# Fourier mixing and a tanh-shrink dense layer on one core: weight conversion in finer steps, with clamp and sums on other engines

## The chip, the cores and the metric

The kernel runs on one core of a Trainium2 chip. A core has five engines that work through their own instruction queues in order and meet only at semaphores: TensorE (PE, matrix products; its weight loads are PEld), VectorE (DVE), ScalarE (ACT), GpSimd (POOL) and SyncE (SP), which here only issues DMA transfers. ScalarE and GpSimd issue DMAs too. The metric is the device time of one execution in microseconds, the median of several runs; lower is better.

## The reference

The input `x` holds 8 batches of 3008 tokens with 256 channels. Every batch is filtered along the sequence in the frequency domain, and the result goes through two dense layers with h - tanh(h) between them:

```python
def _attn_ref(x, filt_r, filt_i):
    X = np.fft.rfft(x, axis=1)
    F = (filt_r + 1j * filt_i)[None, :, :]
    return np.fft.irfft(X * F, n=x.shape[1], axis=1).astype(np.float32)

def _moe_ref(x, w_in, w_out):          # x (24064, 256), w_in (256, 2048), w_out (2048, 256)
    h = x @ w_in
    g = h - np.tanh(h)
    return (g @ w_out).astype(np.float32)
```

The two weight matrices arrive as 64-bit floats, and the kernel reads them as pairs of 32-bit words: each weight's sign, exponent and mantissa are taken apart with integer operations and put together again as a 32-bit float.

## The kernel before

**Fourier part.** The transform of 3008 = 64 x 47 points is done in matrix products. For one batch, `first` (twelve steps, product `pf`, L255) reads x and writes `ct1` to memory; `middle` (seven groups `g` of rows) loads `a2` from `ct1` and a part of the filter (`ft`, from `filt_d`), multiplies (`pa`, L287), applies the filter on VectorE (L292 to L312), multiplies back (`pe`, L322) and writes `ct2`; `last` loads `e2` from `ct2` and makes the tokens of one group (`pu`, L419; `ut`, and the sums `tu` by `combine`). A batch has six groups of tokens.

**Dense part.** A round `U` is one quarter of the hidden channels for one group of tokens; four rounds make a group, 192 rounds make the kernel. Both layers use a scheme of seven products for a 2 x 2 block product: `wu` (first layer) and `wd` (second layer) hold seven blocks, four of which are sums of others, formed by `sums`; the token side is formed by `combine` (four subtractions). In the body for `U`, `up(U)` multiplies by `wu` into the banks x, y and z and gathers `h` with VectorE (L476, L493, L501, L509) and with copies on ScalarE (`s1`, `u2`, `u3`, L459); `shrink(U-1)` works through ScalarE (turn, bend, square: L524, L527, L530) and VectorE (L534), and ends with `combine` on GpSimd, which makes `t`; `down(U-2)` multiplies by `wd` (L578).

**What sets the order.** The order on every engine is the order in which Python emits the instructions. The steps are generators: at fixed places of `up`, `d`, `e`, `s` and `t` advance the other work by one step. `t(k)` for k = 0 to 4 issues stores, takes one step of the Fourier work of later batches if its place in the plan has come (`pos = 20 * c + 5 * u + k`; `planned` spreads the steps of `first` and `middle` over positions: `first(1)` from 6 to 20, `first(2)` from 20 to 34 and `middle(1)` from LEAD = 34 to LAG = 104), advances `late` by two steps, and `copies` (transfers that GpSimd issues to build `filt_d`) by one. `pf`, `pa`, `pe` and `pu` take turns in two banks, t and y; y is also the bank of the second product of `up`, read by L476.

**Weights.** A job is 128 x 512 weights, a quarter is two jobs and then `sums`. `converted` loads the raw words, takes mantissa (`it`), exponent (`pt`) and sign (`st`) on VectorE (L145, L146, L148), makes a float of the mantissa and shifts the exponent's bias on ScalarE (L157, L158), then on VectorE adds the low word (L160), clamps the exponent at 255 (L162), joins it with the sign (L164) and multiplies into the two or three destinations (L171). It yields four times. Three quarters (six jobs) are converted in the prologue by `convert`: four jobs before the loop over the groups of batch 0, two behind it. The other five quarters are converted by `weights_slow` in the first rounds, one job after the other. `sums` stands on GpSimd (L201 to L204), and so does `combine` for every group but the first.

**Buffers.** In the rounds a job's tiles borrow those of the Fourier work (`tiles1`: raw from `ft`, `it` from `xy`, `pt` from `nn`, `st` from `e1`, `ft` from `a2`); two raw loads are begun ahead. In the prologue the stores of `ct2` for batch 0 go through `e1` with two buffers.

Of the kernel before, what the change touches and what calls it, by code (L numbers as in the profile page):

```python
# [27 lines left out]
NX = NH // XH  # L28
# [62 lines left out]
def kernel(  # L91
# [26 lines left out]
    mats = cst.tile([KM, 6 * KM + 8 * KL], F32, name="mats_sb")  # L118
    exp_b = cst.tile([128, 1], F32, name="exp_b")
    groups = [(b, c) for b in range(BATCH) for c in range(NC)]  # L120
    count = cst.tile([1, 1], I32, name="count")
# [11 lines left out]

    def converted(tiles, src, dsts, queue, alone=False):
# [13 lines left out]
        V.tensor_scalar(out=st, in0=hi, scalar1=-2 ** 31, scalar2=None, op0=ALU.bitwise_and)  # L148
        yield

        if alone:
            V.tensor_scalar(out=ft, in0=it, scalar1=2.0 ** -20, scalar2=1.0,
                            op0=ALU.mult, op1=ALU.add)
            V.tensor_scalar(out=pt, in0=pt, scalar1=-896.0, scalar2=0.0,
                            op0=ALU.add, op1=ALU.max)
        else:
            ACT.activation(ft, it, AF.Identity, bias=1.0, scale=2.0 ** -20)  # L157
            ACT.activation(pt, pt, AF.Relu, bias=exp_b)  # L158
        yield
        V.scalar_tensor_tensor(out=ft, in0=lo, scalar=2.0 ** -52, in1=ft,  # L160
                               op0=ALU.mult, op1=ALU.add)
        V.tensor_scalar_min(pt, pt, 255.0)  # L162
        yield
        V.scalar_tensor_tensor(out=pt, in0=pt, scalar=23, in1=st,  # L164
                               op0=ALU.logical_shift_left, op1=ALU.bitwise_or)
        pt = pt.bitcast(F32)
        for cols, dst, sign in dsts:
            f, p = ft[:, cols], pt[:, cols]
            if len(dst.shape) == 3:
                f, p = (v.rearrange("p (h n) -> p h n", h=dst.shape[1]) for v in (f, p))  # L170
            V.scalar_tensor_tensor(out=dst, in0=f, scalar=sign, in1=p, op0=ALU.mult, op1=ALU.mult)  # L171
        yield
# [33 lines left out]
    def begun(tiles, job, alone=False, queue=nc.sync):  # L206
        j = converted(tiles, *job, queue, alone)
        next(j)
        return j

    def weights_slow(tiles, quarters):

        jobs = parts_of(quarters)
        began = [begun(tiles, job) for job in jobs[:2]]
        yield
        for k in range(len(jobs)):
            for _ in began[k]:
                yield
            if k + 2 < len(jobs):
                began.append(begun(tiles, jobs[k + 2]))  # L220
            if k % 2:
                sums(quarters[k // 2])
                yield

# [185 lines left out]
    def last(i, z):  # L410
# [101 lines left out]
    def shrink(U):  # L512
# [20 lines left out]
        def times(k):  # L533
# [216 lines left out]
    with tc.tile_pool(name="tr", bufs=2) as tr, tc.manual_schedule():  # L750

        def tiles1(k, dtype, n):

            tag, bufs = {"raw": ("ft", 2), "it": ("xy", 2), "pt": ("nn", 1), "st": ("e1", 2),
                         "ft": ("a2", 2)}[k]
            return tr.tile([128, n], dtype, tag=tag, bufs=bufs, name=k)

        with tc.tile_pool(name="pro", bufs=1) as pro, \
# [62 lines left out]
            f0 = pro.tile([128, NH, 128], F32, name="f0")  # L821
            V.memset(exp_b, 0.0)
            for t in filt:
                G.memset(t[0:SG, 2:4], 0.0)
# [16 lines left out]

            def convert(k):

                for _ in range(1 if k + 1 < len(jobs) else 0):
                    next(began[k + 1])
                for _ in began[k]:
                    pass
                if k % 2:
                    sums(k // 2)
                if k + 4 < len(jobs):  # L850
                    began.append(begun(tiles0, jobs[k + 4], queue=G))

# [17 lines left out]
            for g in range(last_g + 1):  # L870
# [30 lines left out]
        with tc.tile_pool(name="dn", bufs=2) as dn, \  # L901
# [49 lines left out]
            for U in range(total + 2):  # L951
# [24 lines left out]
                def e():  # L976

                    next(dw, None)

                def s():  # L980
# [3 lines left out]
                def t(k):  # L984
# [76 lines left out]
```

## Time and profile before

| | us |
|---|---|
| median of three runs (2797.88 to 2799.99) | 2798.9 |
| the profiled execution | 2804.2 |
| its span, first to last instruction | 2802.3 |

The busy time of the engines in stretches of the span (us), with the mean granted clock of TensorE and the share of time that the 16 DMA engines were busy:

| stretch | length | PE | DVE | ACT | POOL | PE clock | DMA |
|---|---|---|---|---|---|---|---|
| 0 to 100 | 100 | 58.27 | 56.63 | 26.73 | 41.83 | 0.87 | 0.84 |
| 100 to 200 | 100 | 76.59 | 76.83 | 53.22 | 49.84 | 0.85 | 0.54 |
| 200 to 260 | 60 | 53.28 | 22.68 | 31.61 | 26.90 | 0.91 | 0.64 |
| 260 to 320 | 60 | 59.02 | 44.18 | 37.85 | 40.50 | 1.00 | 0.36 |
| 320 to 1000 | 680 | 675.38 | 423.86 | 435.16 | 334.10 | 1.00 | 0.31 |
| 1000 to 2800 | 1800 | 1779.67 | 1058.76 | 1151.30 | 882.54 | 1.00 | 0.25 |

The prologue ends near 104 us, the first products of the dense part start at 106.27, and the last job of the weights ends at 190.5. In a line of a timeline the columns are the start in us, the duration (of the whole group, where the line ends in x2, x3, x4), the engine, the line of the code, the operation, output and inputs, the shape, and in brackets how long the engine had been idle before and what ended that.

### The profile page before, as it was taken

How to read it: one execution, taken by the hardware profiler on the slowest of the kernel's cores; microseconds unless marked ns; L12 is line 12 of the kernel's file. 1: busy time of each engine (PE TensorE's matmuls, PEld its weight loads, DVE VectorE, ACT ScalarE, POOL GpSimd, SP SyncE). 2: the span in 40 equal slices, each digit the busy share in tenths (PEclk: the TensorE clock that was granted, in tenths of full speed). 3: DMA queues.
4: the chain of work that ended last, by engine and by line, in shares of the span. 5: the costliest groups of instructions: out<-in, count | busy, mean ns of one | idle time of the engine just before them, and what ended most of it. 6: DMA issues, size and time to landing. Idle time of an engine off the chain costs nothing.

```text
span 2802.3 us, 36449 instructions
## 1 busy us (share of the span) xinstructions
PE 2702.2 (96%) x12878; PEld 2375.4 (85%) x12878; DVE 1682.9 (60%) x2076; ACT 1735.9 (62%) x2603; POOL 1375.7 (49%) x1184
## 2 busy tenths in 40 slices
PE   4888999999999999999999999999999999999998
PEld 3677888988889888988889888898888988899886
DVE  4864775666556665656656666566654766554544
ACT  2455666666666666666666666666666666666665
POOL 4355555544445454545455444454544554454452
PEclk8989999999999999999999999999999999999999
DMA  8655323323132332233223331242322222111110
GB/s 235 196 172 143 76 46 84 86 69 83 50 95 75 88 82 59 69 76 103 55 62 74 102 85 47 61 115 66 78 53 69 53 64 54 30 24 33 21 26 18
DMA packets 341378, 215.44 MB, mean 77 GB/s; under 512 B 227736, under 2 KB 300988, under 8 KB 340995
## 3 DMA queue, kind: packets, MB, share of 16 engines
q1 hardware_dynamic: 295740, 151.00, 22.8%
q10 hardware_dynamic: 40071, 52.71, 6.0%
q0 software_dynamic: 5376, 9.33, 1.2%
q8 instruction: 103, 1.69, 0.2%
q14 instruction: 88, 0.72, 0.1%
HBM read 137.83 MB, written 78.12 MB: 77 GB/s over the span
## 4 chain that ended last, share of the span: by engine, by line
PE 89%; DVE 6%; issue 2%; ACT 2%; DMA 1%; SPq 0%; ACTq 0%; POOL 0%; DVEq 0%
PE o L578 38%; PE x L453 22%; PE z L453 11%; PE y L453 5%; PE pa L287 3%; PE pe L322 3%; PE pu L419 3%; PE pf L255 2%; DVE h L534 1%; DVE h L476 1%; DVE h L509 1%; DMA x<-in_x_dram 1%; DVE xy L312 0%; DVE xy L311 0%; PE pe L803 0%
## 5 line engine op out<-in xcount | busy, mean ns | idle before, releaser
L578 PE MATMUL o<-t,wd 128*128 128x256 f32 (+1 forms) x3072 | 776.5, 375 | 0.0
L433 POOL TENSOR_TENSOR t<-h 128x512 f32<-128x512 f32 (+1 forms) x190 | 261.3, 1375 | 883.9 <-DVE h L534 858.8
L534 DVE TENSOR_TENSOR h<-h,y 128x1024 f32<-128x1024 f32 (+1 forms) x384 | 512.9, 1336 | 287.2 <-ACT y L530 286.7
L578 PEld LDWEIGHTS o<-t,wd 128*128 128x128 f32 x3072 | 584.1, 190 | 70.1 <-issue 2.4
L453 PE MATMUL x<-tu,wu 128*128 128x256 f32 (+1 forms) x2304 | 586.1, 377 | 7.0 <-ACT u L459 6.7
L578 PE MATMUL o<-h,wd 128*128 128x256 f32 (+1 forms) x2304 | 584.3, 376 | 3.0 <-DVE h L534 3.0
L453 PEld LDWEIGHTS x<-tu,wu 128*128 128x128 f32 x2304 | 430.9, 190 | 68.5 <-ACT u L459 15.7
L578 PEld LDWEIGHTS o<-h,wd 128*128 128x128 f32 x2304 | 434.8, 191 | 55.0 <-DVE h L534 4.2
L459 ACT COPY s<-x 128x512 f32<-128x512 f32 (+1 forms) x192 | 110.8, 577 | 508.8 <-PE x L453 497.7
L524 ACT ACTIVATE y<-h 128x1024 f32<-128x1024 f32 (+1 forms) x384 | 400.1, 1042 | 12.8 <-ACT a L256 5.6
L527 ACT ACTIVATE y<-y 128x1024 f32<-128x1024 f32 (+1 forms) x384 | 399.2, 1040 | 12.6 <-ACT a L256 0.4
L530 ACT ACTIVATE y<-y 128x1024 f32<-128x1024 f32 (+1 forms) x384 | 399.9, 1041 | 4.6
L493 DVE TENSOR_TENSOR h<-z,u 128x512 f32<-128x512 f32 (+1 forms) x192 | 130.1, 677 | 267.8 <-ACT u L459 266.6
L459 ACT COPY u<-x 128x512 f32<-128x512 f32 (+1 forms) x384 | 219.3, 571 | 87.8 <-PE x L453 66.2
L435 POOL TENSOR_TENSOR t<-h 128x512 f32<-128x512 f32 (+1 forms) x190 | 271.9, 1431 | 0.0
L434 POOL TENSOR_TENSOR t<-h,t 128x512 f32<-128x512 f32 (+1 forms) x190 | 264.6, 1393 | 14.9
L436 POOL TENSOR_TENSOR t<-t,h 128x512 f32<-128x512 f32 (+1 forms) x190 | 267.6, 1409 | 0.0
L501 DVE COPY h<-x 128x512 f32<-128x512 f32 (+1 forms) x192 | 130.4, 679 | 159.5 <-PE x L453 158.9
L453 PE MATMUL x<-ut,wu 128*128 128x256 f32 (+1 forms) x768 | 195.8, 378 | 1.1 <-DVE h L501 1.1
L453 PE MATMUL z<-tu,wu 128*128 128x256 f32 (+1 forms) x768 | 196.3, 378 | 0.0
L453 PE MATMUL z<-ut,wu 128*128 128x256 f32 (+1 forms) x768 | 195.6, 377 | 0.0
L453 PE MATMUL y<-ut,wu 128*128 128x256 f32 (+1 forms) x768 | 194.9, 376 | 0.0
(118 smaller groups left out, 3068.6 us busy)
## 6 DMA issues: line engine op xcount, KB each, us to landing
e<-ct SPq DMA_DIRECT2D x48, 512.0 KB, 4.2
a<-ct SPq DMA_DIRECT2D x48, 480.0 KB, 5.3
ct<-e ACTq DMA_DIRECT2D x96, 240.0 KB, 2.7
ct<-a ACTq DMA_DIRECT2D x84, 256.0 KB, 2.8
x_sb<-in_x_dram SPq DMA_DIRECT2D x161, 128.0 KB, 3.4
ft<-filt SPq DMA_DIRECT2D x42, 480.0 KB, 6.7
out_dram<-ot SPq DMA_DIRECT2D x1248, 16.0 KB, 1.5
gt<-g SPq DMA_DIRECT2D x48, 256.0 KB, 2.8
```

Source lines behind the costliest of these rows:

```text
L433: by.tensor_sub(t[0], b[0][1], b[0][0])
L434: by.tensor_sub(t[1], b[1][1], t[0])
L435: by.tensor_sub(t[2], b[1][1], b[0][1])
L436: by.tensor_sub(t[3], t[1], b[1][0])
L453: nc.tensor.matmul(bank[:, k], wu[:, q - 1, (2 * u + k) * 128:(2 * u + k + 1) * 128], rhs[q - 1], start=(first and k == 0), stop=True, ski ...
L459: ACT.copy(t, X)
L501: V.tensor_copy(h[:, 2, :, 0:w], X)
L524: ACT.activation(y[k], ht[k], AF.Arctan, scale=TURN)
L527: ACT.activation(y[k], y[k], AF.Tanh, scale=BEND)
L530: ACT.activation(y[k], y[k], AF.Square, scale=SCALE, accum_out=y_sums[:, 2 * U + k // 2:2 * U + k // 2 + 1])
L534: V.tensor_mul(ht[k], ht[k], y[k])
L578: nc.tensor.matmul(product(q), wd[:, q - 1, (2 * u + k) * 128: (2 * u + k + 1) * 128], rhs[q - 1][:, k], start=(u == 0 and k == 0 and q == ...
```

## The change

- `converted` yields after every instruction or nearly so (a job took four steps after its load, it takes ten or eleven). The clamp moves from VectorE to ScalarE: `Relu(255 - p)` in place of `min(p, 255)`, so the exponent comes out subtracted from 255; the sign word gets the exponent bits set (a second operation in the same instruction), and the join is an exclusive or in place of an or.
- `sums` moves from GpSimd to VectorE, a step for each of its four subtractions.
- `weights` in the prologue takes jobs in pairs: six steps of both, then the ends of both, then the sums. `late_weights` in the rounds takes six steps of job k, then the end of job k-1; four raw loads are begun ahead. Four steps are taken in each `t` and three in each `e`, 32 in a round.
- While late weights are left (`pending`), `combine` runs on VectorE; after that on GpSimd as before (the last two rounds on VectorE, as before).
- `tiles1` shares the tiles out anew; `e1` of the prologue moves to its own pool with three buffers.
- `first(1)` is planned over positions 2 to 18 and `first(2)` over 18 to 34; `middle(1)` is begun, with its first two loads, at position 27.

```diff
     def converted(tiles, src, dsts, queue):
...
         V.tensor_scalar(out=it, in0=hi, scalar1=0xFFFFF, scalar2=None, op0=ALU.bitwise_and)
+        yield
         V.tensor_scalar(out=pt, in0=hi, scalar1=20, scalar2=0x7FF,
                         op0=ALU.logical_shift_right, op1=ALU.bitwise_and)
-        V.tensor_scalar(out=st, in0=hi, scalar1=-2 ** 31, scalar2=None, op0=ALU.bitwise_and)
-        yield
...
-            ACT.activation(ft, it, AF.Identity, bias=1.0, scale=2.0 ** -20)
-            ACT.activation(pt, pt, AF.Relu, bias=exp_b)
+        yield
+        V.tensor_scalar(out=st, in0=hi, scalar1=-2 ** 31, scalar2=0x7F800000,
+                        op0=ALU.bitwise_and, op1=ALU.bitwise_or)
+        yield
+        ACT.activation(ft, it, AF.Identity, bias=1.0, scale=2.0 ** -20)
+        yield
+        ACT.activation(pt, pt, AF.Relu, bias=exp_b)
+        yield
+        ACT.activation(pt, pt, AF.Relu, bias=cap_b, scale=-1.0)
         yield
         V.scalar_tensor_tensor(out=ft, in0=lo, scalar=2.0 ** -52, in1=ft,
                                op0=ALU.mult, op1=ALU.add)
-        V.tensor_scalar_min(pt, pt, 255.0)
         yield
         V.scalar_tensor_tensor(out=pt, in0=pt, scalar=23, in1=st,
-                               op0=ALU.logical_shift_left, op1=ALU.bitwise_or)
+                               op0=ALU.logical_shift_left, op1=ALU.bitwise_xor)
         pt = pt.bitcast(F32)
         for cols, dst, sign in dsts:
+            yield
...
-        G.tensor_sub(w[:, 4], w[:, 6], w[:, 3])
-        G.tensor_sub(w[:, 5], w[:, 4], w[:, 0])
-        G.tensor_sub(w[:, 2], w[:, 1], w[:, 5])
-        G.tensor_sub(w[:, 6], w[:, 0], w[:, 6])
+        for to, one_in, less in ((4, 6, 3), (5, 4, 0), (2, 1, 5), (6, 0, 6)):
+            V.tensor_sub(w[:, to], w[:, one_in], w[:, less])
+            yield
...
+    pending = [1]
+
+    def weights(tiles, quarters, queue, began):
+
+        jobs = parts_of(quarters)
+        began += [begun(tiles, job, queue) for job in jobs[len(began):4]]
+        yield
+        for k in range(0, len(jobs), 2):
+            for j in (k, k + 1):
+                for _ in range(6):
+                    next(began[j])
+                    yield
+            for j in (k, k + 1):
+                yield from began[j]
+                if j + 4 < len(jobs):
+                    began.append(begun(tiles, jobs[j + 4], queue))
+            yield from sums(quarters[k // 2])
+
+    def late_weights(tiles, quarters):
+
+        jobs = parts_of(quarters)
+        began = [begun(tiles, job) for job in jobs[:4]]
+        yield
+        for k in range(len(jobs) + 1):
+            if k < len(jobs):
+                for _ in range(6):
+                    next(began[k])
+                    yield
+            if k:
+                yield from began[k - 1]
+                if k + 3 < len(jobs):
+                    began.append(begun(tiles, jobs[k + 3]))
+                if k % 2 == 0:
+                    yield from sums(quarters[k // 2 - 1])
+        pending.clear()
...
-        combine(b, [tu[:, k, 0:w] for k in range(4)], G if i else V)
+        combine(b, [tu[:, k, 0:w] for k in range(4)], V if pending else G)
...
-                G if U + 2 < 4 * len(groups) else V)
+                V if pending or U + 2 >= 4 * len(groups) else G)
...
-            tag, bufs = {"raw": ("ft", 2), "it": ("xy", 2), "pt": ("nn", 1), "st": ("e1", 2),
-                         "ft": ("a2", 2)}[k]
-            return tr.tile([128, n], dtype, tag=tag, bufs=bufs, name=k)
+            if k == "raw":
+                raws[0] += 1
+                return tr.tile([128, n], dtype, tag=("ft", "a2")[raws[0] % 2], bufs=2, name=k)
+            if k == "it":
+                halves[0] = tr.tile([128, 2, n], dtype, tag="xy", bufs=2, name="conv")
+            if k in ("it", "ft"):
+                return halves[0][:, int(k == "ft")].bitcast(dtype)
+            if k == "pt":
+                return tr.tile([128, n], dtype, tag="e1", bufs=2, name=k)
+            if not signs:
+                signs.extend([0, tr.tile([128, 2, n], dtype, tag="nn", bufs=1, name=k)])
+            signs[0] += 1
+            return signs[1][:, signs[0] % 2]
...
-                    e1 = tr.tile([KM, 2, DM], F32, tag="e1", bufs=2, name="e1")
+                    e1 = pro.tile([KM, 2, DM], F32, tag="e1", bufs=3, name="e1")
...
-            next(began[0])
-            for k in range(4):
-                convert(k)
+            convert(52)
...
-                    late = weights_slow(tiles1, (4, 3, 5, 6, 7))
+                    signs.clear()
+                    late = late_weights(tiles1, (4, 3, 5, 6, 7))
...
-            for k in range(4, len(jobs)):
-                convert(k)
+            convert(100)
...
-                f = [spread(NX, *((6, 20) if b == 1 else (20, LEAD) if b == 2
+                f = [spread(NX, *((2, 18) if b == 1 else (18, LEAD) if b == 2
...
                 def e():
 
                     next(dw, None)
+                    for _ in range(3):
+                        next(late, None)
...
                     pos = 20 * c + 5 * u + k
+                    if i == 1 and pos == LEAD - 7:
+                        mids[1] = middle(1, z1)
+                        next(mids[1])
...
-                    next(late, None)
-                    next(late, None)
+                    for _ in range(4):
+                        next(late, None)
```

`convert(n)` takes n steps of `weights(tiles0, range(3), G, began)`: 52 steps are two quarters and four steps of the fifth job.

More of the change, by code (lines that the diff above doesn't have):

```diff
@@ L119 @@
     exp_b = cst.tile([128, 1], F32, name="exp_b")
+    cap_b = cst.tile([128, 1], F32, name="cap_b")
     groups = [(b, c) for b in range(BATCH) for c in range(NC)]
@@ L132, with converted @@
     wd = cst.tile([128, 7, DFF // 2], F32, name="wd")
-    def converted(tiles, src, dsts, queue, alone=False):
+    def converted(tiles, src, dsts, queue):
         n = src.shape[-1] * (src.shape[1] if len(src.shape) == 3 else 1)
@@ L145, in converted @@
         V.tensor_scalar(out=it, in0=hi, scalar1=0xFFFFF, scalar2=None, op0=ALU.bitwise_and)
+        yield
         V.tensor_scalar(out=pt, in0=hi, scalar1=20, scalar2=0x7FF,
                         op0=ALU.logical_shift_right, op1=ALU.bitwise_and)
-        V.tensor_scalar(out=st, in0=hi, scalar1=-2 ** 31, scalar2=None, op0=ALU.bitwise_and)
         yield
[L151 to L157, printed above, removed]
-            ACT.activation(pt, pt, AF.Relu, bias=exp_b)
+        V.tensor_scalar(out=st, in0=hi, scalar1=-2 ** 31, scalar2=0x7F800000,
[6 more added lines that the diff above has]
+        ACT.activation(pt, pt, AF.Relu, bias=cap_b, scale=-1.0)
         yield
@@ L200, in sums, with begun @@
         w = (wu if u < 4 else wd)[:, :, 256 * (u % 4):256 * (u % 4) + 256]
-        G.tensor_sub(w[:, 4], w[:, 6], w[:, 3])
-        G.tensor_sub(w[:, 5], w[:, 4], w[:, 0])
-        G.tensor_sub(w[:, 2], w[:, 1], w[:, 5])
-        G.tensor_sub(w[:, 6], w[:, 0], w[:, 6])
-    def begun(tiles, job, alone=False, queue=nc.sync):
-        j = converted(tiles, *job, queue, alone)
+        for to, one_in, less in ((4, 6, 3), (5, 4, 0), (2, 1, 5), (6, 0, 6)):
+            V.tensor_sub(w[:, to], w[:, one_in], w[:, less])
+            yield
+    def begun(tiles, job, queue=nc.sync):
+        j = converted(tiles, *job, queue)
         next(j)
         return j
-    def weights_slow(tiles, quarters):
+    pending = [1]
+    def weights(tiles, quarters, queue, began):
         jobs = parts_of(quarters)
-        began = [begun(tiles, job) for job in jobs[:2]]
+        began += [begun(tiles, job, queue) for job in jobs[len(began):4]]
         yield
-        for k in range(len(jobs)):
-            for _ in began[k]:
-                yield
[L219 to L223, printed above, removed]
+        for k in range(0, len(jobs), 2):
[24 more added lines that the diff above has]
+        pending.clear()
     def load_x(t, b, r, n):
@@ L750 @@
     with tc.tile_pool(name="tr", bufs=2) as tr, tc.manual_schedule():
+        raws, halves, signs = [0], [None], []
         def tiles1(k, dtype, n):
-            tag, bufs = {"raw": ("ft", 2), "it": ("xy", 2), "pt": ("nn", 1), "st": ("e1", 2),
-                         "ft": ("a2", 2)}[k]
-            return tr.tile([128, n], dtype, tag=tag, bufs=bufs, name=k)
+            if k == "raw":
[11 more added lines that the diff above has]
+            return signs[1][:, signs[0] % 2]
         with tc.tile_pool(name="pro", bufs=1) as pro, \
@@ L822 @@
             V.memset(exp_b, 0.0)
+            V.memset(cap_b, 255.0)
             for t in filt:
@@ L840, with convert @@
             turned_rows()
[L842 to L851, printed above, removed]
+            early = weights(tiles0, range(3), G, began)
+            next(early)
+            def convert(n):
+                for _ in range(n):
+                    next(early, None)
             for c in range(3):
```

## The prediction

> **What bounds the kernel now.** I read the page first, engines and the forty slices.
>
> ```profile
> PE 2702.2 (96%) x12878; PEld 2375.4 (85%) x12878; DVE 1682.9 (60%) x2076; ACT 1735.9 (62%) x2603; POOL 1375.7 (49%) x1184
> ...
> PE   4888999999999999999999999999999999999998
> ...
> PEclk8989999999999999999999999999999999999999
> ```
>
> TensorE is the bound almost everywhere: 2702.2 of 2802.3 us, and nearly all of the missing 100 us lies in the first four slices (70 us each). An edit to the first rounds can only win there. So next the table of waits, TensorE alone, first 320 us (total, times, longest):
>
> ```profile
> PE pa L287 <- issue: 15.5, 1, 15.5
> PE pf L255 <- DVE h L476: 13.4, 4, 4.8
> PE pa L287 <- DMA a<-ct: 6.7, 1, 6.7
> PE x L453 <- ACT u L459: 6.3, 4, 3.0
> ```
>
> The 15.5 us (and 18.0 for the first x loads) lie in the prologue, before any weight is needed; the change leaves them. The other three are its targets. In the timeline of the same engine two of them look so:
>
> ```profile
> 188.05 2.07 PE L255 MATMUL pf<-x_sb,f 128*128 128x256 f32 x4 [4.78 <-DVE h L476]
> 189.92 1.91 PE L453 MATMUL z<-tu,wu 128*128 128x256 f32 x4
> ...
> 194.37 1.03 PE L255 MATMUL pf<-x_sb,f 128*128 128x256 f32 x4
> ...
> 239.30 2.03 PE L287 MATMUL pa<-a,mats_sb 120*120 120x256 f32 x4 [6.71 <-DMA a<-ct]
> ```
>
> After a wait of over 4 us the next matmuls take twice their time (2.07 against 1.03 for the same four): each such wait costs some 3.3 us more (1.05 on pf, 0.9 on z, 1.35 on the eight o behind). Why VectorE is late, its own timeline shows, with GpSimd's beside it:
>
> ```profile
> 129.04 0.43 DVE L162 TENSOR_SCALAR pt<-pt 128x512 int32<-128x512 int32 x1
> ...
> 137.79 1.36 DVE L162 TENSOR_SCALAR pt<-pt 128x512 int32<-128x512 int32 x1
> 139.19 1.51 DVE L164 SCALAR_TENSOR_TENSOR pt<-pt,st 128x512 int32<-128x512 int32 x1
> 140.73 2.57 DVE L171 SCALAR_TENSOR_TENSOR wd<-ft,pt 128x256 f32<-128x256 f32 x3
> 143.22 0.61 DVE L476 TENSOR_TENSOR h<-y,s 128x448 f32<-128x448 f32 x1
> ```
>
> ```profile
> 138.94 1.20 POOL L434 TENSOR_TENSOR t<-h,t 128x448 f32<-128x448 f32 x1
> 140.10 1.57 POOL L435 TENSOR_TENSOR t<-h 128x448 f32<-128x448 f32 x1
> ```
>
> The same clamp takes 0.43 us with GpSimd idle and 1.36 beside its combination; the trio L171 takes 2.57 instead of 0.83 (at 149.47). While GpSimd adds, VectorE's conversions stretch, h is late, and TensorE, whose pf needs the bank that h reads, stands still. Last, what VectorE itself waited for between 104 and 192 us:
>
> ```profile
> DVE ft L160 <- ACT ft L157: 8.6, 4, 3.8
> DVE h L493 <- ACT u L459: 4.1, 3, 2.3
> ```
>
> ScalarE works in order: a conversion step that is not ready holds the copy of x behind it, and the reverse.
>
> **The change, part by part.** All sums are against the span of 2802.3 us (the execution took 2804.2; the runs' median is 2798.9; I subtract the gain from the median).
>
> *Prologue, two quarters converted before 52.7 us.* VectorE loses four clamps (0.46 from start to start, 1.8 us) and gets eight sums of 256 columns. A 224-column subtraction takes 0.31 to 0.41 from start to start (L435, L436 at 107.85), so four sums 1.6 us, eight 3.2. ScalarE gets a clamp per job, priced as the Relu beside it (L158, 0.62 with its dependence). What goes with GpSimd's sums: L146, L148, L160 and L162 at 44 to 47 us (0.95, 0.94, 1.21, 0.94 for 0.42, 0.42, 0.69, 0.42) 2.1 us, and L303, L306 and L308 at 54 to 58 us (1.33, 1.63, 1.09 for 1.22, 1.22, 0.69) 0.9. Walking the new order from ScalarE's first free moment (37.03), VectorE comes to the first xy at 52.8 instead of 52.7; the 0.9 behind it remains. From there VectorE runs some 5.2 us per group and sets the end, so -0.9 carries to the first dense round. Bounds: +2 (raws and filters that GpSimd now fetches earlier share the engines with the a2 load that lands at 47.7; 2.4 us of slack cover it) to -3.
>
> *Conversion in the rounds U=0 to 3.* Ten jobs. VectorE gives up ten clamps, 4.6 us, and the stretching: over the conversion rows from 118 to 186 us I add up 17.2 us above the unhindered times. It takes on five quarters of sums (8.0), three combinations of 448 columns (four times 0.64 as L476, 2.5 each, 7.5) and one tu (1.6): 17.1. So it does 63.5 us of work from the end of the first tu (today 108.46; 107.2 in the new order, 0.9 from the prologue, the rest as GpSimd's sums no longer lie beside it) to the first h of U=4: firsts of ten jobs 10.0 (three times 0.33), seconds 20.9 (0.61, 0.72 and 0.76 to 0.83 each), sums 8.0, h 9.4, products L534 6.1, combinations and tu 9.1, rounded. What is unknown is its holes. I walked the new order of the queues by hand, a row's spacing for each instruction. One step of it: at U=0 VectorE is done with `it` of the third job at 112.2; next in its order is h from u3; ScalarE copies u3 after the second job's clamp (111.7) and a pf copy with its issue (112.65), so h starts at 113.2, a hole of 1.0. The pieces of job k+1 now stand ahead of the end of job k, so ScalarE has its input while VectorE finishes the last job, and the 8.6 us that L160 waits for ScalarE today go; new holes come where h waits for ScalarE's copy of x behind three conversion steps (1.0 at U=0, 2.5 at U=1, 1.0 at U=2, 2.3 at U=3). Sum 7.3 with small ones: the h of U=4 is written at 107.2+63.5+7.3=178.0, and its pf starts there instead of 188.05: 10.0 us, the prologue's 0.9 within. Bounds: no holes, 17.3; as many as VectorE has today in these rounds (15.8 in its table of waits less the 1.8 for the first tu, 14.0), 3.3. I take the walk. Three waits of 4 to 4.8 us become several of 1 to 2.8; TensorE waits 1.9 us ahead of U=4's pf, nearer to the 1.49 ahead of 129.47, which slowed nothing, so the 3.3 us of slow clock behind 188.05 go too.
>
> The two waits of 2.6 and 2.8 us in my U=1 may slow the clock: after 2.61 us, the eight pe at 94.61 took 3.12 us and not 1.73, 1.4 more. One of the two is hidden behind the next wait; I take 1 us off, bounds 0 and 2.8.
> The Trainium skill ("TensorE: Matmul & The Clock Gate", "HAM oscillation — how this bites in real kernels") holds that only gaps above about 3.4 us bring the clock down; by it the sum would be 1 us better, and the row of 94.61 speaks against it.
>
> *The load sooner.* middle(1) issues its two loads at position 27, seven positions (some 23 us at 16 us per U) ahead of first use, no longer behind the stores that hold SP from 226.74 to 232.36; ct1 of batch 1 is complete by position 18. The 6.71 us at 239.30 go, and with them 3.2 us of slow clock behind it (pa 1.0, z 0.9, x 0.9, y 0.4). Bounds 0 (something else holds it) and 9.9; 9.9 is taken, as the landing took 6.8 us. What it is moved past on SP are x loads of a few us; they wait only for TensorE's last reads.
>
> *At nothing:* first(1) from position 2, the same pf matmuls in other places, hidden in U=0's waits (cover gone: 0.9 us each); four raws instead of two on SP at 84 us, ahead of the e load that is only issued at 100 (price if they delay it: 1 MB at 198 GB/s, an estimate from that window, 5.3 us); e1 with three buffers.
>
> Sum: 10.0 - 1 + 3.3 + 9.9 = 22.2, so 2798.9 - 22 = 2777.
>
> **The rivals.** The gain is 17.3 - holes + 2.3 (clock) + 9.9 (load), 29.5 less the holes.
> *The holes stay as today* (14.0, and the slow clock behind U=4 with them): 3.3 - 1 + 9.9 = 12 us, 2787. For it: the same three in-order queues hand to each other. Against: the look-ahead of one job.
> *No holes:* 17.3 + 3.3 + 9.9 = 30.5, with no gap to slow the clock, 2768. For it: ScalarE is asked for only some 57 of 71 us there (ten jobs at 1.8, six half shrinks at 3.0, twelve copies at 0.5, fourteen pf copies with issue at 1.0). Against: the walk finds waits on u in every round.
> *The load is not the last thing waited for at 239,* or is held as well: 22.2 - 9.9 = 12 us, 2787. For it: behind a DMA that comes last others may be nearly as late, and the trace names only the last. Against: ScalarE and VectorE stand idle there, 9.9 and 9.5 us, waiting for TensorE.
> *Slower: ScalarE's queue becomes the bound.* Its copies of x (L459), which free TensorE's bank, stand behind three conversion steps now (1.8 us) that wait for VectorE, a pf copy with its issue (1.0) and turn and bend (1.9). If none of it overlaps, eight copies lose 4.7 us each: 37.6 us of holes, a loss of 8, 2807. It decides from 29.5 us of holes on, twice today's. For it: ScalarE gets 6.2 us more. Against: its spare time, above.
> *It doesn't do what it says:* the combinations would stay on VectorE had the flag not been cleared; but in the new instruction order GpSimd's combinations begin again with U=3's, so no chance is kept for it.
>
> **How the numbers follow.** Forecast 0.58, no holes 0.13, holes as today 0.16, load no gain 0.06, slower by the queue 0.07. Range 2766 to 2793: below, no holes and 2 us more of the prologue; above, holes as today with half of the load's gain and a us more of slow clock. About 0.2% (5.6 us) is what a measurement here can tell from nothing, so faster means under 2793.3. The first four cases give 0.93; the two at 2787 lie only 6 us from that line, so I move 0.06 of them across: faster 0.87, same 0.06, slower 0.07.
>
> **What would show it.** In the changed profile: the clamp's successor on ScalarE near 0.6 us; the last conversions at 0.4 to 0.8 us, none at 1.5 to 3.5; the h of U=4 near 178 and the first pa some 22 us before 239; no wait of pa on a DMA; VectorE's holes in U=0 to 3 near 7 us. It is wrong if conversions stay long with GpSimd still, if x waits for ScalarE's u by more than 10 us in these rounds, or if the clock stays low from 110 to 175 us.

## The result and the profile after

| | before | changed |
|---|---|---|
| median of four runs, us | 2799.09 (2797.88 to 2799.99) | 2778.72 (2778.06 to 2780.64) |
| span of the profiled execution, us | 2802.3 | 2776.4 |
| mean granted clock of TensorE in it | 0.987 | 0.992 |

The ratio of changed to before is 0.9929, with a 95% interval of 0.9911 to 0.9946: 20.4 us in the medians. The two profiled executions differ by 25.9 us, because the one of before took 5 us more than its median; nothing shows in which stretch these 5 us lie. All readings below are differences of profiles, and those to the kernel before can be that much too large.

The page of the changed kernel, engines and two rows of the forty slices (a slice is 69 us):

```profile
PE 2690.2 (97%) x12878; PEld 2366.3 (85%) x12878; DVE 1676.3 (60%) x2109; ACT 1746.0 (63%) x2619; POOL 1328.6 (48%) x1136
...
PE   4799999999999999999999999999999999999998
...
PEclk8999999999999999999999999999999999999999
```

The third and fourth slice of TensorE (139 to 278 us) went from 8 to 9 in tenths, the second fell from 8 to 7, and the clock's third went from 8 to 9: the gain lies in the rounds U=2 and later, not in the first. From 320 us on the waits of TensorE are the same in both kernels (16.0 us before, 15.7 now).

The table of waits of TensorE in the first 320 us of the changed kernel (total, times, longest):

```profile
PE x L474 <- ACT u L480: 6.0, 7, 1.3
PE pf L276 <- DMA x_sb<-in_x_dram: 4.8, 3, 3.0
PE pf L276 <- DVE h L497: 4.1, 2, 2.4
PE pe L836 <- DVE nn L329: 3.2, 1, 3.2
```

The wait of pf for h fell from 13.4 to 4.1 us, and the 6.71 us that pa waited for `a` are gone. One line is new: pf waits for its x load three times, 4.8 us. Nothing in the forecast had it.

The timeline of TensorE at the places shown of before:

```profile
122.95 1.10 PE L276 MATMUL pf<-x_sb,f 128*128 128x256 f32 x4 [3.03 <-DMA x_sb<-in_x_dram]
...
159.18 1.89 PE L276 MATMUL pf<-x_sb,f 128*128 128x256 f32 x4 [2.38 <-DVE h L497]
...
179.58 1.13 PE L276 MATMUL pf<-x_sb,f 128*128 128x256 f32 x4 [1.74 <-DVE h L497]
...
218.73 1.03 PE L308 MATMUL pa<-a,mats_sb 120*120 120x256 f32 x4
```

The pf of U=4 is the line at 179.58: idle 1.74 and not 4.78, at full clock, 8.5 us sooner than at 188.05. The first pa at 218.73 starts without any wait, 20.6 us sooner than at 239.30.

VectorE's timeline, with the same rows as before and the two kinds of work that moved to it:

```profile
115.17 1.68 DVE L202 TENSOR_TENSOR wd<-wd 128x256 f32<-128x256 f32 x4
...
129.77 0.62 DVE L514 TENSOR_TENSOR h<-z,u 128x448 f32<-128x448 f32 x1 [6.44 <-ACT u L480]
...
139.16 0.62 DVE L455 TENSOR_TENSOR t<-h,t 128x448 f32<-128x448 f32 x1
...
159.76 0.83 DVE L171 SCALAR_TENSOR_TENSOR wd<-conv,pt 128x256 f32<-128x256 f32 x3
...
178.85 0.68 DVE L497 TENSOR_TENSOR h<-y,s 128x512 f32<-128x512 f32 x1
```

The trio L171 takes its unhindered 0.83 us (2.57 at 140.73 before), the four sums take 1.68, and one subtraction of a combination takes 0.62 on VectorE where GpSimd took 1.20 to 1.57. The one long hole is 6.44 us, and the h that TensorE's U=4 needs starts at 178.85. The table of what VectorE waited for between 104 and 192 us no longer has a row for L160, the step that waited 8.6 us for ScalarE:

```profile
DVE h L514 <- ACT u L480: 14.0, 5, 6.4
DVE tu L455 <- ACT ut L443: 1.9, 2, 1.5
```

Of the 14.0, 5.0 lie behind the h of U=4.

Why the x loads were late begins in SP's own timeline (issue start, time of the issue), with one row of GpSimd's below it:

```profile
109.19 0.86 SPq L950 DMA_DIRECT2D filt<-zero  x1
...
110.95 0.51 SPq L248 DMA_DIRECT2D x_sb<-in_x_dram  x1
...
114.41 0.61 SPq L254 DMA_DIRECT2D x_sb<-in_x_dram  x1
```

```profile
108.63 0.53 POOL L948 MEMSET zero<- 128x512 f32 x1 [29.76 <-DVE conv L160]
```

The x loads for the third pf (118.06), the first of them issued at 110.95, stand in SP's queue behind the store of zero rows into the filter. That store waits for a clearing on GpSimd (108.63), and the cleared tile takes the buffer in which the first raw words of the late weights lie: GpSimd stood idle 29.76 us until VectorE had read them at L160. The clearing holds more than SP. The copies that build the filter stand behind it in GpSimd's queue, and 18 of them are issued between 109.16 and 122.77. From 116 to 124 us the 16 DMA engines are busy all the time (share 1.01 and 1.07 in the two halves). The long wait, 3.03 us, is that of the fourth pf (122.95): its last x load was issued at 114.41 and landed at 122.82, 8.4 us later. In the kernel before, no x load of this stretch whose landing the trace tells took more than 4.5 us. So the chain is: raw tile, clearing, then zero store and filter copies released together with the loads, crowded DMA engines, x load, pf at 122.95, ScalarE's copy of pf, ScalarE's copies of x behind it, the hole of 6.44 us at 129.77.

### The profile page after: what moved, and what is told of

It reads as the page before. It is cut to its first block, busy times and chain, and to the rows that moved or that the text cites. A ratio compares the mean times of both kernels' runs of the same rounds, so it can differ in the third digit from the quotient of the medians.

```text
span 2776.4 us, 36436 instructions
## 1 busy us (share of the span) xinstructions
PE 2690.2 (97%) x12878; PEld 2366.3 (85%) x12878; DVE 1676.3 (60%) x2109; ACT 1746.0 (63%) x2619; POOL 1328.6 (48%) x1136
## 4 chain that ended last, share of the span: by engine, by line
PE 89%; DVE 5%; ACT 2%; issue 2%; DMA 2%; ACTq 0%; SPq 0%; POOL 0%; DVEq 0%
PE o L599 38%; PE x L474 22%; PE z L474 11%; PE y L474 5%; PE pa L308 4%; PE pe L343 3%; PE pu L440 3%; PE pf L276 2%; DVE h L555 1%; DVE h L530 1%; DMA x<-in_x_dram 1%; DVE h L497 1%; DVE xy L333 0%; DMA ct<-a 0%; DVE xy L332 0%
## 5 line engine op out<-in xcount | busy, mean ns | idle before, releaser
L454 POOL TENSOR_TENSOR t<-h 128x512 f32<-128x512 f32 (+1 forms) x187 | 257.1, 1375 | 940.9 <-DVE h L555 915.9
L456 POOL TENSOR_TENSOR t<-h 128x512 f32<-128x512 f32 (+1 forms) x187 | 268.0, 1433 | 0.0
```

The lines of the kernel that those rows point to most:

```text
L454: by.tensor_sub(t[0], b[0][1], b[0][0])
L456: by.tensor_sub(t[2], b[1][1], b[0][1])
```

## The experiments

To compare kernels by place, I use three marks of each profiled execution: the first product of the rounds (`pu`), the start of the h of U=4 on VectorE, and one and the same output transpose 95 to 110 us behind it (273.78 in the changed kernel). Section 1 runs from the first mark to the second, section 2 from the second to the third. The marks do not enclose the same work: the number of TensorE's matmuls in section 1, given in the table, differs with the order, and only both sections together hold the same 717 in every kernel. So the sum is what compares kernels with different counts. The start of `pu` differs between executions (101.1 to 106.7, and 109.6 in e8), and between two executions of the changed kernel by 2.5 us, so lengths of sections say more than times of day. Ratios of e1 to e11 are to the kernel before on the same chip, five to eleven runs each.

| kernel | pu | section 1 (matmuls) | section 2 | both | median, us | ratio (95%) |
|---|---|---|---|---|---|---|
| before | 104.45 | 82.87 (264) | 110.07 | 192.94 | 2799.09 | 1 |
| changed | 101.80 | 77.05 (276) | 94.93 | 171.98 | 2778.72 | 0.9929 (0.9911 to 0.9946) |
| e1 before + load sooner | 103.88 | 82.42 (264) | 105.12 | 187.54 | 2796.66 | 0.9988 (0.9979 to 0.9997) |
| e2 changed, load as before | 102.37 | 77.35 (276) | 102.18 | 179.53 | 2788.35 | 0.9959 (0.9945 to 0.9972) |
| e3 changed, first from 6 | 101.08 | 74.79 (264) | 102.34 | 177.13 | 2785.88 | 0.9946 (0.9933 to 0.9960) |
| e4 changed, adds on GpSimd | 101.85 | 73.97 (262) | 97.32 | 171.29 | 2781.75 | 0.9933 (0.9920 to 0.9947) |
| e5 before, adds on VectorE | 106.67 | 77.30 (264) | 106.00 | 183.30 | 2794.45 | 0.9982 (0.9973 to 0.9991) |
| e6 changed, clamp on VectorE | 104.22 | 77.55 (276) | 94.93 | 172.48 | 2782.09 | 0.9932 (0.9918 to 0.9945) |
| e7 changed, no look-ahead | 105.76 | 82.71 (274) | 94.96 | 177.67 | 2785.44 | 0.9942 (0.9929 to 0.9956) |
| e8 changed, zero rows early | 109.55 | 74.98 (276) | 94.95 | 169.93 | 2780.34 | 0.9923 (0.9910 to 0.9937) |
| e9 changed, zero rows from a tile of their own | 103.02 | 72.81 (276) | 94.95 | 167.76 | 2777.10 | 0.9925 (0.9912 to 0.9939) |
| e10 finer steps alone | 103.37 | 72.31 (255) | 107.97 | 180.28 | 2788.82 | 0.9962 (0.9949 to 0.9976) |
| e11 the changed kernel again | 104.33 | 76.28 (276) | 94.97 | 171.25 | 2780.63 | 0.9935 (0.9922 to 0.9949) |

Three chips served: e1, e2, e4 and e5 ran on one, e3, e6, e7 and e8 on a second, e9, e10 and e11 on a third. The kernel before took 2799.79, 2800.92 and 2798.80 us on them, so the ratios, and not the medians, compare kernels of different chips.

### The load alone, and the change without it (e1, e2)

e1 puts the early begin of `middle(1)` into the kernel before; e2 takes it out of the changed kernel.

```diff
                     pos = 20 * c + 5 * u + k
+                    if i == 1 and pos == LEAD - 7:
+                        mids[1] = middle(1, z1)
+                        next(mids[1])
```

> The kernel before, with the two first loads of middle(1) begun at position 27 and nothing else. Forecast's theory: the 6.71 us wait of pa on the a load near 239 us goes, and the 3 to 4 us of slow clock behind it; about 10 to 11 us, 2788 to 2789. Rival (something else is nearly as late there): a new wait in the same place, 2794 or more.

> The changed kernel with middle(1) begun at position 34 as before. Forecast's theory: the wait of pa on the load comes back, 10 to 11 us, about 2789. Rival (the earlier end of the conversions had made the load harmless): under 2782.

Measured: taking it out (e2) lengthens section 2 from 94.93 to 102.18 us, 7.3, and the ratio from 0.9929 to 0.9959 (8.4 us of 2799; the intervals just touch). Putting it into the kernel before (e1) brings 5.0 us of section 2 and only 3.4 us of the time. In e2 pa waits for `a` again (5.36 us, at 225.13). In e1 this wait went, but a new one came some 22 us sooner; so the time of the rival came true, by another wait than the one it named. The timelines of e1, TensorE and then ScalarE:

```profile
216.55 1.69 PE L453 MATMUL x<-tu,wu 128*128 128x256 f32 x4 [3.28 <-ACT u L459]
```

```profile
215.55 0.33 ACTq L257 DMA_DIRECT2D ct<-a  x1
215.92 0.58 ACT L459 COPY u<-x 128x512 f32<-128x512 f32 x1 [3.69 <-DMA ft<-filt]
```

ScalarE's store of ct1 at 215.55 was held until the early load of `ft` had landed on another queue, and the copy of x, which TensorE needs, stood behind the store. The packed trace says why: it has the completion semaphore of every transfer, SP's and ScalarE's transfers take eight of them in turn, and the store uses the same one (113) as the `ft` load issued at 207.32, eight transfers ahead of it in the program. In the changed kernel the transfer that takes the semaphore of the `ft` load next is an x load of SP's (204.70), and ScalarE isn't held by it; its hold of 3.36 us at 205.82 is a copy of pf that waits for an earlier store of ct, at a moment when TensorE needs nothing from it. What a load begun sooner is worth depends on what stands in the queues at the moment it is under way, down to which transfer comes to share its semaphore.

### first from position 6 again (e3)

```diff
-                f = [spread(NX, *((2, 18) if b == 1 else (18, LEAD) if b == 2
+                f = [spread(NX, *((6, 20) if b == 1 else (20, LEAD) if b == 2
```

> The changed kernel with first(1) planned over positions 6 to 20 and first(2) over 20 to 34, as before. Forecast's theory: worth nothing, 2778.7 within 2. Theory from the changed profile: beginning sooner made pf wait for x loads (4.8 us of waits, and the 6.4 us hole of VectorE behind them); without it these waits go and VectorE's holes fall from 10.9 to about 7: 2774 to 2777.

Measured: section 1 becomes 2.3 us shorter (74.79), section 2 becomes 7.4 us longer (102.34), both together 5.2 us longer, and the ratio is 0.9946 for 0.9929: 4.8 us, with overlapping intervals. Neither theory had that. Section 1 holds twelve matmuls fewer here and section 2 twelve more, so a part of either difference is work that crossed the mark. In section 2 ScalarE's store collides with the `ft` load again, as in e1, and by the same semaphore (a copy of x at 202.70 waits 3.85 us, TensorE 3.47).

Set beside e2 and e10, the two edits form a square. Both sections together are 180.28 us with neither edit (e10, whose adds and clamp also stand where they stood before), 177.13 with the load alone (e3), 179.53 with `first` alone (e2) and 171.98 with both. So the load alone brings 3.2 us, `first` alone 0.8, and the two together 8.3: they do not stand free of each other. The ratios say the same (0.9962, 0.9946, 0.9959, 0.9929), though neighbours' intervals overlap. e3 has no wait of pf for x; that these waits alone make the 2.3 us of section 1 is not shown.

### The adds back to GpSimd, and the adds alone to VectorE (e4, e5)

e4 leaves everything of the change but the engine of the late sums and combinations. e5 moves just these in the kernel before, as long as late weights are left.

```diff
-            V.tensor_sub(w[:, to], w[:, one_in], w[:, less])
+            (V if u < 3 else G).tensor_sub(w[:, to], w[:, one_in], w[:, less])
...
-        combine(b, [tu[:, k, 0:w] for k in range(4)], V if pending else G)
+        combine(b, [tu[:, k, 0:w] for k in range(4)], G if i else V)
```

> The changed kernel with the sums of the late quarters and all combinations but the first back on GpSimd; steps, clamp and load stay. Accounting of the forecast: VectorE sheds some 17 us of adds and its conversions stretch by up to 17 us again, so within 3 us of 2778.7. Rival (what GpSimd does to VectorE is the cause of the long conversion): conversions of 1.4 to 3.5 us again and waits of 4 us ahead of pf; 6 us or more lost, 2785 to 2790.

> The kernel before with the sums of the late quarters, and the combinations while late weights are left, on VectorE; coarse steps, clamp on VectorE and late load stay. Accounting of the forecast: VectorE's work stays about the same (17 us of adds for 17 us of stretching), so within 3 us of 2799. Rival (GpSimd beside VectorE is the cause): 5 to 9 us gained, 2790 to 2794.

Measured: e4 has the stretching back, as the rival had it, and loses almost nothing by it, as the forecast's accounting had it. VectorE's timeline of e4, and GpSimd's beside it:

```profile
151.97 3.52 DVE L171 SCALAR_TENSOR_TENSOR wd<-conv,pt 128x256 f32<-128x256 f32 x3
155.53 1.24 DVE L146 TENSOR_SCALAR conv<-raw 128x512 int32<-128x512 int32 x1
```

```profile
151.42 1.50 POOL L454 TENSOR_TENSOR t<-h 128x448 f32<-128x448 f32 x1 [1.36 <-DVE h L555]
153.01 1.19 POOL L455 TENSOR_TENSOR t<-h,t 128x448 f32<-128x448 f32 x1
154.16 1.18 POOL L456 TENSOR_TENSOR t<-h 128x448 f32<-128x448 f32 x1
155.30 1.18 POOL L457 TENSOR_TENSOR t<-t,h 128x448 f32<-128x448 f32 x1
```

Three multiplications that take 0.83 us alone take 3.52 here, 1.17 each, which is what one subtraction of GpSimd takes (1.18): the two engines take turns. The Trainium skill ("SBUF — State Buffer", "Who interferes with whom") says just that of a VectorE instruction with two inputs in SBUF beside a GpSimd instruction that reads SBUF, the second to begin being held until the first is done; this trace agrees. Yet section 1 is 73.97 us, 3.1 shorter than in the changed kernel, though pf waits 3.82 us for h in it (159.15); 2.4 of the 3.1 us come back in section 2. Fourteen of TensorE's matmuls have crossed the mark, and in section 2 TensorE waits less than in the changed kernel (1.3 us for 3.0), so the two differences are for the most part work that moved. Both sections together are 171.29 us for 171.98, and in time e4 is at 0.9933, no different from 0.9929.

e5 says the other half: in the coarse kernel, moving the adds away does shorten section 1, 82.87 to 77.30 with the same 264 matmuls, and the time by 5.0 us (0.9982), at the lower edge of what the rival gave. So in the order of the kernel before the adds on GpSimd did make h late; with finer steps they cost nothing that these runs can tell. The two remedies don't add up.

### The clamp back on VectorE (e6)

```diff
-        ACT.activation(pt, pt, AF.Relu, bias=cap_b, scale=-1.0)
...
+        V.tensor_scalar_min(pt, pt, 255.0)
```

The sign and the join (xor to or) go back with it.

> The changed kernel with the clamp back on VectorE (min, behind the low word's add) and an or for the join. Forecast's theory: VectorE gets 4.6 us in the ten late jobs and 1.8 in the prologue, ScalarE loses 6: up to 5 us slower, 2780 to 2784, as VectorE sets the pace there. Rival (ScalarE's queue sets the pace, its clamp stands ahead of the copies of x): 2 us or more faster, under 2777.

Measured: section 1 77.55 for 77.05, section 2 the same, ratio 0.9932 for 0.9929. From 100 to 200 us VectorE is busy 78.49 us for 72.86, ScalarE 59.20 for 67.91, and the waits of VectorE between 104 and 192 us shrink by about what its work grows (19.0 to 13.8). Neither the loss of the forecast nor the gain of the rival came. The move of the clamp is worth nothing that these runs can tell.

### No look-ahead (e7)

Finer steps stay, but a job is taken to its end before the next is begun.

```diff
-        for k in range(len(jobs) + 1):
-            if k < len(jobs):
-                for _ in range(6):
-                    next(began[k])
-                    yield
-            if k:
-                yield from began[k - 1]
...
+        for k in range(len(jobs)):
+            yield from began[k]
```

> The changed kernel with late_weights taking one job to its end before the next is begun (same steps, same engines, same four raw loads ahead). Theory now: the look-ahead is what spares VectorE its waits for ScalarE; the waits of L160 for L154 come back, 6 us or more slower, 2785 or more. Rival (fine steps alone do it): within 2 us of 2778.7.

Measured: section 1 is 82.71 us, as long as before the change (82.87). VectorE's waits of e7 between 104 and 192 us:

```profile
DVE conv L160 <- ACT conv L154: 7.2, 3, 6.5
DVE pt L163 <- ACT pt L158: 5.2, 5, 2.8
```

These are the 8.6 us of before again, now 12.4. The ratio is 0.9942 for 0.9929: 3.6 us, less than the 6 expected, with overlapping intervals, where both sections together are 5.7 us longer. So the waits and the sections show what the look-ahead is worth; the time alone does not. No run has the look-ahead with coarse steps.

### Finer steps alone (e10)

The changed kernel with adds on GpSimd (as in e4), the clamp on VectorE (as in e6), `first` from 6 (as in e3) and the load as before (as in e2): what is left of the change is the steps, the look-ahead and the buffers.

> The changed kernel with sums and combinations on GpSimd, the clamp on VectorE, first(1) from position 6 and middle(1) at 34, all as before: what is left is the finer steps with the look-ahead, four raw loads ahead and the buffers. Theory that the look-ahead is the cause of the shorter first rounds: pu to the h of U=4 in 74 to 78 us (82.9 before), time about 2790. Theory of the forecast's opening (GpSimd's adds beside VectorE): 82 or more, time 2795 or more.

Measured: section 1 is 72.31 us, the shortest of all, with the stretching in it (a trio of L170 takes 3.53 us); but it holds 21 matmuls fewer than the changed kernel's and nine fewer than before, and section 2, 107.97, holds them instead, with 5.7 us of pa's wait for `a`. Both together are 12.7 us shorter than before. The ratio is 0.9962, 10.6 us: half of the whole gain. The other half is what the load and the earlier `first` bring together (0.9962 to 0.9929, 9.2 us). How the first half divides among steps, look-ahead, raw loads ahead and buffers, no run separates.

### The zero rows out of the way (e8, e9), and the changed kernel again (e11)

e8 writes the zero rows in the prologue, ahead of the late weights. e9 keeps their place in SP's queue but clears a small tile of its own at the start and stores it by broadcast in seven transfers:

```diff
+    zero = cst.tile([64, 64], F32, name="zero")
...
-                zero = tr.tile([128, 2 * DM], F32, tag="a2", bufs=2, name="zero")
-                G.memset(zero, 0.0)
...
+                for g in range(n + 1):
+                    m = SG if g < n else 1
+                    nc.sync.dma_start(dram(filt_d, (g * KM * 4 + 2) * DM,
+                                           [[4 * DM, m], [64, 8], [1, 64]]),
+                                      zero[0:m].unsqueeze(1).to_broadcast([m, 8, 64]))
```

> The changed kernel with the zero rows of filt_d written in the prologue, so that SP's x loads of first(1) no longer stand behind a memset that waits for the first raw tile. Theory: the x load for the third pf is issued some 8 us sooner and its waits shrink; 1 to 4 us faster, 2775 to 2778. Rival (these x loads are late for the load of the DMA engines, not for the queue): within 1 us of 2778.7.

> The changed kernel with the zero rows of filt_d written from a small tile that is cleared at the start and kept, in the old place of SP's queue: nothing there waits for a raw tile. Theory: the 4.8 us of pf's waits for x loads go, as in the run that wrote them in the prologue, and the e load is not delayed; first rounds (pu to the h of U=4) 75 us and not 77, 2 to 3 us faster than the changed kernel on the same chip. Rival (the engines' load makes x late): no difference.

> The changed kernel itself, unedited, for comparison on the same chip: 20 us under the kernel before, ratio 0.993.

Measured: both remove every wait of pf for x. In both, `pu` comes to wait for the load of `e` from ct2 instead, longer than in the changed kernel (0.74 us); TensorE's timeline of e8, then of e9:

```profile
109.55 2.98 PE L440 MATMUL pu<-gt,e 128*128 128x128 f32 x16 [4.39 <-DMA e<-ct]
```

```profile
103.02 1.97 PE L441 MATMUL pu<-gt,e 128*128 128x128 f32 x16 [2.10 <-DMA e<-ct]
```

e9's waits of TensorE from 104 to 320 us (lines stand one lower in this kernel):

```profile
PE x L475 <- ACT u L481: 7.7, 8, 2.0
PE pf L277 <- DVE h L498: 5.2, 3, 2.4
```

The row of x loads is gone, VectorE's hole in U=1 is 2.57 us for 6.44, and section 1 is 72.81 us, for 76.28 of the changed kernel on the same chip (e11). e9's median is 2777.10 (2776.05 to 2779.91), e11's 2780.63 (2779.88 to 2782.31). That is 3.5 us, the same as the section shows; the ratios' intervals overlap. e9 has the lowest median of all these kernels; by their ratios e8 (0.9923) and e9 (0.9925) are level, and the profiled execution of e8 was its slowest of five.

The expectations set SP's queue against the load of the DMA engines, and these two runs do not part them: with no clearing in the way, GpSimd issues its 18 filter copies in the prologue (79.7 to 94.6 in e9), and the share of the DMA engines between 116 and 124 us falls to 0.79 and 0.76. For the longest wait the times of issue decide. The x load of the fourth pf was issued 12.6 us behind `pu` in the changed kernel and 11.9 behind it in e9 (114.94), nearly the same; yet e9's fourth pf, at 120.20, did not wait for it:

```profile
120.20 1.13 PE L277 MATMUL pf<-x_sb,f 128*128 128x256 f32 x4 [1.12 <-DVE h L498]
```

So there it was the time under way (8.4 us) and not the place in SP's queue. The filter copies are not the only crowd: e4 issues five of them in that stretch, and its fourth pf still waits 2.42 us. Which of the transfers released together matter, no run separates.

## Why the prediction was right, and which steps were not

The time came out at 2778.7, with 2777 forecast, and faster. By its own steps:

- **Prologue, 0.9 us.** The first xy came at 53.93, not 52.8, and VectorE wasn't the cause: it had been done since 51.8 and waited 2.10 us for pa. `pu` came 2.65 us sooner, but the prologue's loads, which landed sooner in that execution, make about 1.4 of it (first conversion at 28.98, 30.41 before). As `pu` moves by 2.5 us between two executions of the changed kernel, this term stays open.
- **VectorE's work, 63.5 us.** Right: 62.65 from the end of the first tu to the h of U=4. The price list (sums 1.6 for 1.68, combinations 0.64 for 0.62, all conversions unstretched, ScalarE's clamp 0.62 to 0.72) held.
- **VectorE's holes, 7.3 us.** Too few: 10.9. One hole of 6.44 makes the difference; the forecast put 2.5 at U=1. Its cause is the step "at nothing" below; in e9, without the late x loads, that hole is 2.57. The h of U=4 starts at 178.85 for 178.0 forecast only since work began 1.9 us sooner than forecast (105.3 for 107.2).
- **pf of U=4, 10.0 us.** 8.5 by the profile. The idle time ahead of it (1.74 for 1.9) and the full clock behind it are as forecast, and the offset between the two kernels grows to 12.7 us by the transpose at 213.31, so the slow clock gave 4.2 for 3.3. The 1 us taken off for the clock in U=1 can't be read by itself; slow matmuls are there (132.05). It can hardly be more: the changed kernel has three stretches at half rate in section 1 and the same kernel in e11 has one, and the section is 77.05 and 76.28 us.
- **The load, 9.9 us.** The offset grows by 10.9 around it, but the load alone isn't the cause of all: with `first` from 6 beside it (e3 against e10) it brings 3.2 us, and on top of the earlier `first` (e2) 7.3 us of section 2, by time 8.4.
- **"At nothing: first(1) from position 2."** This step failed: on top of the load it is worth 5.2 us over both sections, 4.8 by time (e3), with a loss in section 1 and a larger gain in section 2. The step looked at TensorE alone, where the pf matmuls are indeed hidden, and not at what each step issues: its x loads come to stand behind the zero store and among the crowd of transfers that the clearing releases, and the order of its transfers decides whether a ct1 store in ScalarE's queue takes the semaphore of the `ft` load. So the right total rests in part on errors that cancel, and that is luck: against the 5.2 us that were not counted stand the 1.5 us missing at the pf of U=4, where the longer holes end up, and the 2.6 us missing of the load (7.3 for 9.9).
- **"Four raws instead of two" at nothing.** Wrong, through the buffers more than through the e load that was named: the raw words took the buffers of the cleared tile (e9: 3.5 us by the medians). `pu` waits 0.74 us for the e load, where it didn't before.
- **The opening picture,** GpSimd's adds stretching VectorE's conversions as the cause of the late h, was right of the kernel before (e5) and did not carry the change: its accounting had said itself that 17.2 us shed and 17.1 taken on leave nothing. What shortened section 1 is finer steps with the look-ahead, which the forecast had as the removal of L160's waits: without the look-ahead (e7) these waits are back and the section is as long as before, and the steps, with look-ahead and buffers and nothing else (e10), bring 12.7 of the 21.0 us of both sections.

The rivals: "holes as today" is nearest to e7, whose VectorE waits 19.2 us between 104 and 192, and e7's ratio puts it at 2782.7 for the 2787 given. "The load no gain" is e2's condition, 2787.4 by its ratio for 2787. Neither holds of the change itself. "Slower by ScalarE's queue" needed 29.5 us of holes, and there were 10.9; x waited for u by 6.0 us, where more than 10 would have told against the forecast.

## What to carry to other kernels

When two engines pass pieces of a job back and forth in order, beginning the next piece ahead of the end of this one can be worth more than moving work between them: here finer steps with a look-ahead, and the buffers for them, brought half of the gain, while two moves of work (clamp, adds) brought nothing measurable on top of it. A transfer or a step that is begun sooner is to be followed through each queue it enters, with every older entry that waits for something: a clearing that waited for a shared buffer held a store of zeros and the filter copies, and these then crowded the loads that TensorE needed. And gains of edits to one schedule are to be tested together as well as alone, as the load was worth 3.4 us in one order and 8.4 in the other.

## What the runs showed of the hardware

- The clock does not follow the single gap. After an idle time of 3.03 us the pf at 122.95 ran at full rate (1.10 us), and the pf at 132.05, after 1.23 us, took 2.05. After 2.38 us the one at 159.18 took 1.89. The Trainium skill ("TensorE: Matmul & The Clock Gate", "What's actually happening") has the clock set by windows of about 3.4 us that run freely, not by the gap itself; that the same gap may or may not be punished fits this. That it takes a gap above 3.4 us, as the Trainium skill has it on the same page ("HAM oscillation — how this bites in real kernels"), does not hold for the row at 159.18.
- The granted clock of these traces shows more. Every stretch at half rate between `pu` and the third mark is 3.41 us long or a multiple of it (before: four of 6.83 and one of 10.24; changed: three of 3.41, at 111.62, 132.10 and 159.41). In the 3.41 us ahead of each of the changed kernel's three, TensorE was busy for 1.25, 1.09 and 1.03 us, and ahead of the five before for between 0.00 and 1.12. In the 3.41 us from 118.45, the changed kernel's emptiest that was not followed by a fall, it was busy for 1.47, since the idle 3.03 us ahead of 122.95 lie across two such stretches. Where TensorE then worked without a pause the half rate ended after 3.41 us, as in the changed kernel; where it didn't, it lasted longer. The limit is not a sharp one here: in e8 a fall follows a stretch in which TensorE was busy for 1.53.
- A DMA that ScalarE issues can hold ScalarE for another queue's transfer: 3.69 us in e1, 3.85 in e3, until the `ft` load had landed, although the store has nothing to do with that load's data. In both the store uses the completion semaphore of the `ft` load (113), and ScalarE waits for it ahead of the issue.
